# Two attention blocks on one core: K and V issued once per batch step, wq in blocks of columns, Q in half-octet blocks, 97 remainder tiles transposed by DMA

## The chip, the cores and the metric

The kernel runs on one core of a Trainium2 chip. The metric is device time in microseconds (us) of one execution. Before the change three runs took 774.91, 777.09 and 790.09 us; the median is 777.09. The profiled execution took 776.1 us.

## The reference

Two independent problems, A and B, have the same shapes, and their outputs are joined along the last axis. For each:

```python
B, Sq, D = 16, 80, 576
Hq, Hkv, Sk, Dh = 32, 16, 512, 128          # two query heads share a K/V head
q = (x @ wq).reshape(B, Sq, Hq, Dh).transpose(0, 2, 1, 3)
scores = einsum("bhqd,bhkd->bhqk", q, repeat(k_cache, 2)) * Dh ** -0.5
o = einsum("bhqk,bhkd->bhqd", softmax(scores), repeat(v_cache, 2))
out = o.transpose(0, 2, 1, 3).reshape(B, Sq, Hq * Dh) @ wo
```

All inputs are bf16.

## The kernel before

**Units.** The work is cut into 128 units U, 64 for each problem. A unit is one batch element with four K/V heads, that is eight query heads. Eight units that share the same columns of wq and the same half of the batch make an "octet" (`goct`, 16 of them). The two query heads of a K/V head give 160 query rows. 128 of these make one full tile, and the 32 rows that are left over from each of the four heads are put together into one "remainder" tile of 128 rows. So a unit has five score tiles of 128 x 512: one remainder tile (k = 0) and four full ones (k = 1 to 4).

**The steps of a unit.** TensorE projects Q for a whole octet: for each of eight heads, five chained matmuls over the 576 input columns (line 566), for 480 and for 160 columns in turn (`QB = ((0, 6), (6, 2))`, line 520). ACT or DVE evicts and scales the result to qT (lines 577, 578). Scores come from line 689 (full tiles) and line 675 (remainders: four matmuls of 32 columns beside each other in the array, two units at a time). Then DVE takes the negative maximum of each row (698), ACT the exponential with the row sums (702), DVE the reciprocal (708), and POOL normalises in place (711). TensorE transposes the probabilities in four blocks (717), and DVE evicts them to pT (723 for remainders, 725 for full tiles). TensorE multiplies with V (762), ACT evicts to oT (778). The output projection (815) runs over 16 heads at a time in two groups of eight matmuls, and its sums go through `acc` (827, 835) to the output tile (843) and out (849).

**Remainders by DMA.** For some units, listed by ranges in `RSEL` (line 54), the remainder tile isn't transposed by TensorE: SP issues a DMA transpose from p_sb to pT (line 729). Each range of `RSEL` is (first unit, end, which of U mod 4). In this kernel these are 75 of 128 units. There the remainder gets a reciprocal of its own (`RG`, line 53), ahead of the one for the four full tiles.

**Loads.** K is loaded and transposed by DMA from SP (641), into five buffers (`NK`). V is loaded from ACT's queue (645), into four buffers (`NV`); the first four come from SP. wq comes in pieces from SP (539, 542), into two slots; wo comes from SP (606), in four pieces for each half of its columns. x of problem A is loaded (478) and transposed on TensorE (493); x of B is transposed by DMA (512), one of five chunks at a time. SP also stores the output.

**What sets the order.** Nothing is ordered by hand. Every step is an operation of a planner (`_Sched`, lines 117 to 350) with a key, a stream, a duration and the resources that it reads and writes. The planner (`arrange`, line 161) walks through time with its own durations and DMA costs, takes for each engine the ready operation with the lowest priority number, and so fixes each engine's program, the banks of PSUM, and which of ACT and DVE evicts Q. Options of an operation that matter here: `ahead` lowers the priority number, `after` and `lag` hold an operation back in the plan until some time after a "mark" (the PV step of a unit and head; mark 4U + g is head g of unit U) was planned. These holds are only the plan's. In the program that comes out (`finalize`, line 284) an instruction waits only for the semaphores of the data and buffers that it uses; but each engine, SP included, runs its program strictly in order.

**Names that the change touches.** `LA` (line 14) is how many score tiles the scores run ahead of the transposes. `NPA` and `NPR` are the numbers of probability buffers for full and for remainder tiles. `QL0`, `QL1`, `QL2` are how many units the projection of an octet leads its use. `NQ` is the number of octets for which qT has room. `RDK`, `RDO` place the DMA transposes of remainders in SP's order. `WQR`, `XR`, `WOR` place the loads of wq, x of B and wo. `NWARM2` is the number of dummy matmuls (line 453) between the first and the second block of x at the start.

Of the kernel before, what the change touches and what calls it, by code (L numbers as in the profile page):

```python
# [6 lines left out]
BF16 = mybir.dt.bfloat16  # L7
# [5 lines left out]
GR = 2  # L13
LA = 10
NK = 5
NV = 4
NPA = 8
NPR = 4
NPT = 3
NS = 16  # L20
QL0 = 15.0
QL1 = 10.0
KC = 2.1
VK = 8.0
# [16 lines left out]
VN = 1  # L41
VLAG = 2.0
VAF = (None, None, None, None)
STENG = "sp"
# [3 lines left out]
NVS = 4  # L48
# [16 lines left out]
OPSPLIT = 2  # L65
XLD = ((-100.0, -60.0), (-25.0, -24.9))
XH = 0.0
WQ1 = -16.8
WQ1B = 0.02
# [3 lines left out]
LPC = 29.0  # L73
WOR = (((4.0, 1.5), (12.0, 1.5)), ((9.5, 2.0), (17.0, 1.0)), ((9.5, 2.0), (17.0, 1.0)), ((9.5, 2.0), (17.0, 1.0)))
WQR = (-12.0, 2.0)
XR = (-14.0, 2.0)

# [39 lines left out]
class _Sched:  # L117
# [43 lines left out]
    def arrange(self):  # L161
# [72 lines left out]
        while left:  # L234
# [118 lines left out]
def bass_concat_heads__gqa_block_cached__gqa_block_cached__near_ridge_kernel(  # L353
# [27 lines left out]
    with ExitStack() as es:  # L381
# [91 lines left out]
        for half in range(NPP):  # L473
            x_ap = probs[0][0]
            for part, (k0, k1) in enumerate(XP):
                def em_ldx(e, x_ap=x_ap, half=half, k0=k0, k1=k1):
                    src = x_ap.rearrange("b s d -> (b s) d")[half * NROW + k0 * 128:half * NROW + k1 * 128, :]
                    return e.dma_start(xs[:, half * NRT + k0:half * NRT + k1, 0:D],
                                       src.rearrange("(k p) d -> p k d", p=128))

                S.add("sp", XLD[half][part], em_ldx,
                      writes=[R(("xs", half * NRT + k_), 0) for k_ in range(k0, k1)], dsem="d_x%d%d" % (half, part),
                      name="ldx%d.%d" % (half, part), stream="x", dur=0.5, cost=XC * (k1 - k0))
            for blk in range(NRT):
                rb = half * NRT + blk
                vb = S.bank("M0" if half == 0 else "M1")
                x = (XA + 0.5 * blk if blk < 2 else XA + 4.0 + 0.5 * blk) if half == 0 else XH + 0.8 * blk

# [30 lines left out]

        QB = ((0, 6), (6, 2))  # L520
        for goct in range(NG):
# [3 lines left out]
            wsl = wv % 2  # L525
            qsl = goct % NQ
            u0 = goct * 8
            pieces = () if half else ((0, 512), (512, 1024)) if goct < 2 else ((0, 1024),)
            for pi, (c0, c1) in enumerate(pieces):
                st0 = u0 - lead[goct]  # L530
                t_ld = 5.0 * st0 - 20.0 if goct > 1 else (-90.0, WQ1)[goct] + (10.0, WQ1B)[goct] * pi
                fr = (c1 - c0) / 1024.0
                dsem = "d_wqs" if goct == 0 and pi == 0 else "d_wqt" if goct == 1 and pi == 0 else "d_wq%d" % wsl
                eng = ("act", "sp")[goct] if goct < 2 else WENG
                strm = "wqa" if goct == 0 else "wqs" if goct == 1 else "wq"
                for k0, k1 in (((0, 4), (4, 5)) if goct < 2 else ((0, 1), (1, 2), (2, 3), (3, 4), (4, 5))):
                    def em_ldw(e, wq_ap=wq_ap, q=q, wsl=wsl, c0=c0, c1=c1, k0=k0, k1=k1):
                        if k0 == 4:
                            return e.dma_start(wq_sb[64:128, wsl, 4, c0:c1],
                                               wq_ap[512:576, q * 1024 + c0:q * 1024 + c1])  # L540
                        src = wq_ap[k0 * 128:k1 * 128, q * 1024 + c0:q * 1024 + c1]
                        return e.dma_start(wq_sb[:, wsl, k0:k1, c0:c1], src.rearrange("(c p) n -> p c n", p=128))

                    S.add(eng, t_ld + 0.01 * k0, em_ldw,
                          writes=[R(("wq", wsl, ck, p_), wv) for ck in range(k0, k1)
                                  for p_ in ([pi] if len(pieces) == 2 else [0, 1])], dsem=dsem,
                          name="ldw%d.%d.%d" % (goct, pi, k0), stream=strm, dur=0.5,
                          cost=(0.12 + 0.2 * WQC * (k1 - k0) if k0 < 4 else 0.4) * fr,
                          after=int(4 * (st0 + WQR[0] + WQR[1] * k0)) if goct > 1 else None,
                          lag=WLAG if goct > 1 else 0.0)  # L550

            for i in range(8):
                for c in range(2):
                    if goct == 0:
                        b0, nb = ((0, 2), (2, 6))[c]
                        x = -LA - ((6.0, 3.6), (1.2, 0.5))[i // 4][c] + (0.6 if i < 4 else 0.05 if c == 0 else 1.2) * (i % 4)
                    else:
                        b0, nb = QB[c]
                        x = 5.0 * (u0 - lead[goct] + i) + (3.6 if c == 0 else 1.6)
                    n0, n1 = b0 * SQ, (b0 + nb) * SQ  # L560
# [11 lines left out]

                    def em_qev(e, en, qsl=qsl, b0=b0, nb=nb, n0=n0, n1=n1, col=col, vb=vb):
                        dst = qT[:, qsl, b0:b0 + nb, col:col + 80]
                        src = ps[:, vb.phys, 0:n1 - n0].rearrange("p (b s) -> p b s", b=nb)
# [5 lines left out]
                    if prob:  # L581
                        xr += [R(("xT", half, "t", ck), 1) for ck in range(1, 5)]
                    S.add("pe", x, em_qp,
                          reads=[R(("wq", wsl, ck, i // 4), wv) for ck in range(5)] + [R(("wqz",), 0)] + xr,
                          writes=[R(vb, 0)] + [R(("qT", qsl, bl, i), goct) for bl in range(b0, b0 + nb)],
                          name="qp%d.%d.%d" % (goct, i, c), stream="Q",
                          dur=_mm(5, n1 - n0), lat=0.2, alloc=[vb])
                    big = n1 - n0 > 200
                    S.add(("act", "dve"), x + 0.4, em_qev, reads=[R(vb, 0)],
                          writes=[R(("qT", qsl, bl, i), goct) for bl in range(b0, b0 + nb)],  # L590
                          name="qev%d.%d.%d" % (goct, i, c), stream="qev",
# [40 lines left out]
        for U in range(NSU):  # L632
# [3 lines left out]
            _, kc_ap, vc_ap, _, _ = probs[prob]  # L636
            ks, vs, pts, qsl = U % NK, U % NV, U % NPT, goct % NQ

# [16 lines left out]
            rdma = any(a_ <= U < b_ and U % 4 in m_ for a_, b_, m_ in RSEL)  # L655
            for k in range(5):
# [11 lines left out]
                if k == 0:  # L668
                    group.append((U, vb, ks, qsl, bl, goct))
                    if len(group) == gsize[U]:  # L670
                        def em_qkr(e, group=tuple(group)):
                            last = None
                            for _, vb_, ks_, qsl_, bl_, _ in group:
                                for g4 in range(4):
                                    last = e.matmul(ps[32 * g4:32 * g4 + 32, vb_.phys, :],  # L675
                                                    lhsT=qT[:, qsl_, bl_, g4 * 160 + 128:g4 * 160 + 160],
                                                    rhs=kT[:, ks_, :, g4 * 128:(g4 + 1) * 128],
# [3 lines left out]
                        S.add("pe", Qof[(group[0][0], 0)] - LA + 0.0, em_qkr,  # L681
                              reads=[R(("qT", g_[3], g_[4], i), g_[5]) for g_ in group for i in (1, 3, 5, 7)]
                              + [R(("kT", g_[2]), g_[0]) for g_ in group],
# [3 lines left out]
                else:  # L687
                    def em_qk(e, gl=gl, vb=vb, ks=ks, qsl=qsl, bl=bl):
                        return e.matmul(ps[:, vb.phys, :], lhsT=qT[:, qsl, bl, gl * 160:gl * 160 + 128],  # L689
                                        rhs=kT[:, ks, :, gl * 128:(gl + 1) * 128], start=True, stop=True)  # L690

                    S.add("pe", tq, em_qk,
                          reads=[R(("qT", qsl, bl, 2 * gl), goct), R(("qT", qsl, bl, 2 * gl + 1), goct),
                                 R(("kT", ks), U)],
# [234 lines left out]
```

## Time and profile before

| what | value |
|---|---|
| median of three runs | 777.09 us |
| profiled execution | 776.1 us, of which the profile's span is 774.4 us |
| TensorE (PE) busy | 767.0 us, 7,958 matmuls |
| DVE busy | 682.7 us |
| ACT busy | 605.9 us |
| POOL busy | 433.3 us |
| moved by DMA | 170.36 MB, a mean of 220 GB/s |
| remainder transposes by DMA | 75 |

The span runs from the first to the last instruction; the time of the execution has 1.7 us more around it. An engine's busy time counts each moment once, in which at least one of its instructions runs. Matmuls overlap in their pipeline, so the sum of their durations is larger than the busy time; what a matmul costs is read from the distance between two starts. A line such as L717 is line 717 of the kernel. In a timeline, "x4" stands for four instructions merged into one line, with the start of the first and the time to the end of the last.

### The profile page before, as it was taken

To read this page: it belongs to the slowest core of one execution; us is meant where nothing else is said; L and a number is where in the kernel's file an instruction comes from. 1 tells how busy PE (TensorE), PEld (TensorE's weight loads), DVE (VectorE), ACT (ScalarE), POOL (GpSimd) and SP (SyncE) were. 2 spreads that over 40 slices of the span, in tenths; PEclk is the share of its full clock that TensorE was granted. 3 is DMA by queue.
4 is the path that set the end of the run, shared out by engine and by line. 5 is a ranking of instruction groups with operands and counts; after the bars stand their busy time and mean duration, and the time that the engine had idled before them with its cause. 6 is when DMAs were issued, how large, how long until landed. Compare 5 with 4: busy or idle time off the path is not lost.

```text
span 774.4 us, 21088 instructions
## 1 busy us (share of the span) xinstructions
PE 767.0 (99%) x7958; PEld 560.4 (72%) x7958; DVE 682.7 (88%) x1590; ACT 605.9 (78%) x1704; POOL 433.3 (56%) x647
## 2 busy tenths in 40 slices
PE   9999999999999999999999999999999999999998
PEld 5577677777767677777777777677777777767786
DVE  4999989888898989989898899988888888999982
ACT  1778978888888888777777777878788877887860
POOL 1465656566655556555655555655556565565660
PEclk9999999999999999999999999999999999999999
DMA  9998999999999999999999999999999989999931
GB/s 252 225 252 192 252 250 237 230 195 233 205 210 208 220 265 247 267 269 223 200 214 187 206 224 246 249 239 235 218 220 211 200 202 209 246 239 259 249 84 31
DMA packets 411811, 170.36 MB, mean 220 GB/s; under 512 B 317632, under 2 KB 408256, under 8 KB 411712
## 3 DMA queue, kind: packets, MB, share of 16 engines
q1 hardware_dynamic: 345024, 102.83, 74.8%
q10 hardware_dynamic: 66688, 66.20, 28.8%
q8 instruction: 64, 1.05, 0.6%
q14 instruction: 35, 0.29, 0.1%
HBM read 87.46 MB, written 2.95 MB: 117 GB/s over the span
## 4 chain that ended last, share of the span: by engine, by line
PE 88%; DVE 10%; ACT 1%; issue 0%; POOL 0%; ACTq 0%
PE ps L566 20%; PE ps L815 20%; PE ps L762 16%; PE ps L717 14%; PE ps L689 12%; DVE negmax L698 6%; PE ps L675 4%; DVE pT L725 2%; DVE qT L578 1%; ACT p_sb L702 1%; PE ps L438 0%; DVE pT L723 0%; PE ps L453 0%; PE ps L493 0%; DVE xT L497 0%
## 5 line engine op out<-in xcount | busy, mean ns | idle before, releaser
L711 POOL TENSOR_SCALAR p_sb<-p_sb,rinv 128x512 bf16<-128x512 bf16 x640 | 430.9, 695 | 319.9 <-DVE rinv L708 319.8
L702 ACT ACTIVATE p_sb<-ps,negmax 128x512 bf16<-128x512 f32 x640 | 441.4, 693 | 92.7 <-DVE negmax L698 79.9
L698 DVE TENSOR_REDUCE negmax<-ps 128x1 f32<-128x512 f32 x640 | 427.9, 678 | 11.5 <-PE ps L689 7.0
L725 DVE COPY pT<-ps 128x512 bf16<-128x512 bf16 x512 | 209.4, 411 | 20.1 <-PE ps L717 19.2
L762 PE MATMUL ps<-pT,v_sb 128*128 128x160 bf16 x2048 | 219.9, 233 | 1.1 <-issue 0.4
L717 PE MATMUL ps<-ident,p_sb 128*128 128x128 bf16 x2260 | 218.0, 219 | 2.0 <-POOL p_sb L711 1.1
L566 PE MATMUL ps<-xT,wq_sb 128*128 128x480 bf16 (+1 forms) x1280 | 213.0, 300 | 0.1
L762 PEld LDWEIGHTS ps<-pT,v_sb 128*128 128x128 bf16 x2048 | 159.0, 98 | 51.5 <-ACT oT L778 4.5
L689 PE MATMUL ps<-kT,qT 128*128 128x512 bf16 x512 | 190.4, 379 | 0.0
L717 PEld LDWEIGHTS ps<-ident,p_sb 128*128 128x128 bf16 x2260 | 159.5, 98 | 40.1 <-DVE pT L725 7.5
L815 PE MATMUL ps<-wo_sb,oT 128*128 128x288 bf16 x1280 | 171.2, 286 | 0.2
L566 PEld LDWEIGHTS ps<-xT,wq_sb 128*128 128x128 bf16 x1280 | 106.7, 98 | 62.7 <-DVE qT L578 2.7
L815 PEld LDWEIGHTS ps<-wo_sb,oT 128*128 128x128 bf16 x1280 | 122.2, 98 | 36.2 <-issue 1.5
L778 ACT CAST oT<-ps 128x320 bf16<-128x320 f32 x256 | 108.8, 425 | 28.2 <-PE ps L762 27.7
L702 ACT ACTIVATION_READ_ACCUMULATOR p_sb<-ps,negmax 128x1 f32 x640 | 129.1, 202 | 0.0
L578 DVE TENSOR_SCALAR qT<-ps 128x480 bf16<-128x480 f32 (+1 forms) x129 | 71.6, 555 | 17.1 <-PE ps L566 15.7
L577 ACT ACTIVATE qT<-ps 128x160 bf16<-128x160 f32 (+1 forms) x127 | 48.0, 378 | 27.7 <-PE ps L566 27.0
L689 PEld LDWEIGHTS ps<-kT,qT 128*128 128x128 bf16 x512 | 49.4, 98 | 4.5 <-ACT p_sb L702 2.1
L843 DVE TENSOR_TENSOR osb<-ps,acc 128x288 bf16<-128x288 f32 x40 | 18.2, 455 | 25.1 <-PE ps L815 24.5
L675 PE MATMUL ps<-kT,qT 128*32 128x512 bf16 x512 | 39.6, 384 | 0.1
L708 DVE RECIPROCAL rinv<-rowsum 128x4 f32<-128x4 f32 (+2 forms) x203 | 33.0, 165 | 5.1 <-ACT p_sb L702 5.0
L723 DVE COPY pT<-ps 128x512 bf16<-128x512 bf16 x53 | 21.9, 413 | 3.4 <-PE ps L717 3.2
(19 smaller groups left out, 48.5 us busy)
## 6 DMA issues: line engine op xcount, KB each, us to landing
v_sb<-in_B_v_cache_dram ACTq DMA_DIRECT2D x64, 512.0 KB, 5.1
v_sb<-in_A_v_cache_dram ACTq DMA_DIRECT2D x60, 512.0 KB, 5.3
wo_sb<-in_A_wo_dram SPq DMA_DIRECT2D x16, 288.0 KB, 4.5
wo_sb<-in_B_wo_dram SPq DMA_DIRECT2D x16, 288.0 KB, 5.2
wq_sb<-in_B_wq_dram SPq DMA_DIRECT2D x16, 256.0 KB, 5.5
out_dram<-osb SPq DMA_DIRECT2D x40, 72.0 KB, 3.5
v_sb<-in_A_v_cache_dram SPq DMA_DIRECT2D x4, 512.0 KB, 5.3
wq_sb<-in_A_wq_dram SPq DMA_DIRECT2D x8, 256.0 KB, 5.4
```

The source lines that it names most:

```text
L566: last = e.matmul(ps[:, vb.phys, 0:n1 - n0], lhsT=wq_sb[:, wsl, ck, i * 128:(i + 1) * 128], rhs=xT[:, half, ck, n0:n1], start=(ck == 0), s ...
L578: return e.tensor_scalar(dst, src, SCALE, None, op0=AluOpType.mult)
L675: last = e.matmul(ps[32 * g4:32 * g4 + 32, vb_.phys, :], lhsT=qT[:, qsl_, bl_, g4 * 160 + 128:g4 * 160 + 160], rhs=kT[:, ks_, :, g4 * 128: ...
L689: return e.matmul(ps[:, vb.phys, :], lhsT=qT[:, qsl, bl, gl * 160:gl * 160 + 128], rhs=kT[:, ks, :, gl * 128:(gl + 1) * 128], start=True, ...
L698: return e.tensor_reduce(negmax[:, si:si + 1], ps[:, vb.phys, :], axis=AX.X, op=AluOpType.max, negate=True)
L702: return e.activation(p_sb[:, psl, :], ps[:, vb.phys, :], AF.Exp, bias=negmax[:, si:si + 1], scale=1.0, accum_out=rowsum[:, ss, k:k + 1])
L711: return e.tensor_scalar(p_sb[:, psl, :], p_sb[:, psl, :], rinv[:, ss, k:k + 1], 1.0, op0=AluOpType.mult, op1=AluOpType.mult)
L717: last = e.transpose(psb[:, vt.phys, j * 128:(j + 1) * 128], p_sb[:, psl, j * 128:(j + 1) * 128], ident[:])
L725: return e.tensor_copy(pT[:, pts, :, 0:4, gl * 32:gl * 32 + 32], psb[:, vt.phys, 0:512].rearrange("p (j h c) -> p j h c", j=4, h=4))
L762: last = e.matmul(ps[:, vo.phys, off:off + 160], lhsT=v_sb[:, vs, gl, j * 128:(j + 1) * 128], rhs=pT[:, pts, j, :, gl * 32:gl * 32 + 32], ...
L778: return e.copy(dst, src)
L815: last = e.matmul(ps[:, vb.phys, 0:DC], lhsT=oT[:, hi, rb * 128:(rb + 1) * 128], rhs=wo_sb[:, hi, c3 * DC:(c3 + 1) * DC], start=(hi == 0), ...
```

## The change

- **Look-ahead and buffers.** `LA` goes from 10 to 13 score tiles, with two more buffers for full probability tiles and one more for remainders.
- **K and V.** Each unit's K load is held in the plan until the mark that lies 27 heads before the unit's first PV step (`KPH`, from unit 10 on), and each V load until the one 11 heads before (`VPH`, from unit 14 on). So they are planned once per unit, instead of as soon as a buffer is free.
- **wq.** From the third octet on, a load of wq comes as four blocks of 256 columns with all four full row chunks, plus one piece for the last 64 rows. Before, it came as four row chunks with all 1,024 columns, plus the same piece. Dependencies follow the blocks of columns, so a block can be replaced as soon as its two heads are projected.
- **Order with reserves.** In the plan, a DMA counts as landed later than before by a fixed reserve (`XM`: 6.0 for wo and wq, 4.0 for remainder transposes, 3.0 for x, 2.0 for K and V). The priorities `PTO`, `OEO`, `OVO`, `QEO`, `RCO`, which were 0, get values (`QEO` is used nowhere).
- **Q.** An octet is projected in two blocks of four units (320 columns each) instead of six and two units; the second block follows the first by at least 0.7 units. qT has five half-octet blocks instead of three octets.
- **Remainders.** `RSEL` now names 97 units: the odd ones of units 18 to 23 are new, the odd ones now go through from 46 to 61, and from 62 to 125 it is every unit (22 more in all).
- **Start.** The second warm-up has four matmuls instead of eight, and the first transposes of x stand closer together.

The diff, cut to its core:

```diff
-LA = 10
+LA = 13
-NPA = 8
-NPR = 4
+NPA = 10
+NPR = 5
-QL1 = 10.0
+QL1 = 11.0
-QL2 = 10.0
+QL2 = 10.3
-NQ = 3
+NQB = 5
+QSH = 0.7
+QS0 = 12.0
-NWARM2 = 8
+NWARM2 = 4
+VPH = 11
+VU0 = 14
+KPH = 27
+KU0 = 10
+KLAG = 0.0
+XM = dict(wo=6.0, wq=6.0, wqb=6.0, RT=4.0, V=2.0, K=2.0, x=3.0)
-RSEL = ((24, 46, (0, 1, 2, 3)), (46, 50, (1, 3)), (62, 70, (1, 3)), (70, 76, (0, 1, 2, 3)), (76, 94, (1, 3)), (94, 126, (0, 1, 2, 3)))
+RSEL = ((18, 24, (1, 3)), (24, 46, (0, 1, 2, 3)), (46, 62, (1, 3)), (62, 126, (0, 1, 2, 3)))
-RDK = 3.0
-RDO = 6.0
+RDK = 2.0
+RDO = 10.0
-PTO = 0.0
-OEO = 0.0
-OVO = 0.0
-QEO = 0.0
-RCO = 0.0
+PTO = 1.0
+OEO = 4.0
+OVO = 8.0
+QEO = 6.0
+RCO = 2.0
...
-                o.done = t_ + DLAT
+                o.done = t_ + DLAT + XM.get(o.stream, 0.0)
...
-        qT = sb("qT", [128, NQ, 8, 640], BF16)
+        qT = sb("qT", [128, 4 * NQB, 640], BF16)
...
-        QB = ((0, 6), (6, 2))
+        def qpos(goct, bl):
+            return (2 * goct + bl // 4) % NQB * 4 + bl % 4
+
+        QB = ((0, 4), (4, 4))
...
-                for k0, k1 in (((0, 4), (4, 5)) if goct < 2 else ((0, 1), (1, 2), (2, 3), (3, 4), (4, 5))):
+                if goct < 2:
+                    parts = ((0, 4, c0, c1), (4, 5, c0, c1))
+                else:
+                    parts = tuple((0, 4, 256 * j, 256 * j + 256) for j in range(4)) + ((4, 5, 0, 1024),)
...
-                          after=int(4 * (st0 + WQR[0] + WQR[1] * k0)) if goct > 1 else None,
+                          after=int(4 * (sp_ + at)) if goct > 1 else None,
...
-                        x = 5.0 * (u0 - lead[goct] + i) + (3.6 if c == 0 else 1.6)
+                        x = 5.0 * (u0 - lead[goct] + i + c * max(QSH, lead[goct] - QS0)) + 1.6
...
-                  dsem="d_k%d" % ks, name="ldk%d" % U, stream="K", dur=1.8, cost=KC, xp=True)
+                  dsem="d_k%d" % ks, name="ldk%d" % U, stream="K", dur=1.8, cost=KC, xp=True,
+                  after=4 * U - KPH if U >= KU0 else None, lag=KLAG if U >= KU0 else 0.0)
...
-                      lag=VLAG if U >= NVS else 0.0, after=VAF[U] if U < 4 else None)
+                      lag=VLAG if U >= NVS else 0.0, after=VAF[U] if U < 4 else 4 * U - VPH if U >= VU0 else None)
```

More of the change, by code (lines that the diff above doesn't have):

```diff
@@ L67 @@
 XH = 0.0
+XB = 4.0
 WQ1 = -16.8
@@ L482, in bass_concat_heads__gqa_block_cached__gqa_block_cached__near_ridge_kernel @@
                       writes=[R(("xs", half * NRT + k_), 0) for k_ in range(k0, k1)], dsem="d_x%d%d" % (half, part),
-                      name="ldx%d.%d" % (half, part), stream="x", dur=0.5, cost=XC * (k1 - k0))
+                      name="ldx%d.%d" % (half, part), stream="x0", dur=0.5, cost=XC * (k1 - k0))
             for blk in range(NRT):
@@ L535, in bass_concat_heads__gqa_block_cached__gqa_block_cached__near_ridge_kernel @@
                 strm = "wqa" if goct == 0 else "wqs" if goct == 1 else "wq"
-                for k0, k1 in (((0, 4), (4, 5)) if goct < 2 else ((0, 1), (1, 2), (2, 3), (3, 4), (4, 5))):
-                    def em_ldw(e, wq_ap=wq_ap, q=q, wsl=wsl, c0=c0, c1=c1, k0=k0, k1=k1):
-                        if k0 == 4:
[L539 to L548, printed above, removed]
-                          after=int(4 * (st0 + WQR[0] + WQR[1] * k0)) if goct > 1 else None,
+                sp_ = st0 if goct < 2 else u0 - 16 - lead[goct - 2] + max(QSH, lead[goct - 2] - QS0)
@@ L589, in bass_concat_heads__gqa_block_cached__gqa_block_cached__near_ridge_kernel @@
                     S.add(("act", "dve"), x + 0.4, em_qev, reads=[R(vb, 0)],
-                          writes=[R(("qT", qsl, bl, i), goct) for bl in range(b0, b0 + nb)],
+                          writes=[R(("qT", qpos(goct, bl), i), goct) for bl in range(b0, b0 + nb)],
                           name="qev%d.%d.%d" % (goct, i, c), stream="qev",
@@ L681, in bass_concat_heads__gqa_block_cached__gqa_block_cached__near_ridge_kernel @@
                         S.add("pe", Qof[(group[0][0], 0)] - LA + 0.0, em_qkr,
-                              reads=[R(("qT", g_[3], g_[4], i), g_[5]) for g_ in group for i in (1, 3, 5, 7)]
+                              reads=[R(("qT", g_[3], i), g_[4]) for g_ in group for i in (1, 3, 5, 7)]
                               + [R(("kT", g_[2]), g_[0]) for g_ in group],
```

43 lines of the change are left out of this document (26 added, 17 removed).

## The prediction

> **What bounds the kernel now.** I read the page's busy times and chain first, then the groups by line, the waits, stretches of 20 us, and the timelines of TensorE and of SP's queue.
>
> ```profile
> PE 767.0 (99%) x7958; PEld 560.4 (72%) x7958; DVE 682.7 (88%) x1590; ACT 605.9 (78%) x1704; POOL 433.3 (56%) x647
> ...
> PE 88%; DVE 10%; ACT 1%; issue 0%; POOL 0%; ACTq 0%
> ```
>
> TensorE is busy nearly always and carries the chain. Busy could still hide slack, so look at the distances between starts:
>
> ```profile
> 107.53 0.44 PE L762 MATMUL ps<-pT,v_sb 128*128 128x160 bf16 x4
> 107.81 0.39 PE L717 MATMUL ps<-ident,p_sb 128*128 128x128 bf16 x4
> 108.03 0.44 PE L762 MATMUL ps<-pT,v_sb 128*128 128x160 bf16 x4
> 108.31 0.39 PE L717 MATMUL ps<-ident,p_sb 128*128 128x128 bf16 x4
> 108.53 0.38 PE L689 MATMUL ps<-kT,qT 128*128 128x512 bf16 x1
> ```
>
> The columns are start, length and matmuls. A group of four transposes starts 0.22 us before its successor: 55.7 ns a matmul, 128 columns at 2.4 a ns plus some 2.5. Of 160 columns one takes 69 ns, of 288 122, of 480 202, of 512 216: all pure streaming. Added up by form, all 7,958 starts account for 754 of the 770 us between the first and last start (two 0.1 us turns per remainder group included). So only some 16 us are left to win: 3 before the second block of x, and 13 in all that follows. Of those 13, gaps over 0.1 us make 8.4. What they look like:
>
> ```profile
> 543.64 0.44 PE L762 MATMUL ps<-pT,v_sb 128*128 128x160 bf16 x4 [0.20 <-issue]
> ```
> ```profile
> 495.98 0.40 PE L717 MATMUL ps<-ident,p_sb 128*128 128x128 bf16 x4 [0.23 <-DVE pT L725]
> 496.21 0.38 PE L689 MATMUL ps<-kT,qT 128*128 128x512 bf16 x1
> 496.43 0.72 PE L762 MATMUL ps<-pT,v_sb 128*128 128x160 bf16 x8
> 497.45 0.40 PE L717 MATMUL ps<-ident,p_sb 128*128 128x128 bf16 x4 [0.31 <-POOL p_sb L711]
> ```
>
> The first is a PV that waits for a remainder tile transposed by DMA (unit 89; it landed at 543.55). The others wait for pT's eviction and for a probability tile that POOL had just normalised. Why was the DMA late? SP's queue, with the length of each issue:
>
> ```profile
> 527.12 6.45 SPq L641 DMA_TRANSPOSE kT<-in_B_k_cache_dram  x1
> 533.62 0.58 SPq L542 DMA_DIRECT2D wq_sb<-in_B_wq_dram  x1
> 534.25 4.73 SPq L641 DMA_TRANSPOSE kT<-in_B_k_cache_dram  x1
> 539.08 1.21 SPq L729 DMA_TRANSPOSE pT<-p_sb  x1
> ```
>
> Unit 89's buffer was free at 530.26, but SP stood for 4 to 6 us on each K load's issue and reached the transpose at 539.08. The rings are nearly full here. What they can move:
>
> ```profile
> 280.00:300.00 20.00, 20.00 (x213) 14.78 (x211) 17.99 (x42) 16.94 (x49) 12.17 (x19) 1.00 1.15 265
> 300.00:320.00 20.00, 19.92 (x221) 14.57 (x214) 19.30 (x47) 17.01 (x48) 11.19 (x18) 1.00 1.19 261
> 320.00:340.00 20.00, 20.00 (x213) 14.93 (x212) 18.32 (x41) 16.02 (x46) 12.62 (x19) 1.00 1.19 281
> ...
> 520.00:540.00 20.00, 20.00 (x215) 14.87 (x213) 16.59 (x40) 15.59 (x44) 12.42 (x19) 1.00 1.11 237
> 540.00:560.00 20.00, 19.80 (x215) 14.75 (x214) 17.84 (x42) 15.97 (x46) 10.12 (x15) 1.00 1.15 229
> ```
>
> The last column is GB/s: 269 over 280 to 340 with PE untroubled. The granted clock, third from last, is 1.00. DMA is the second bound, and the change leans on it.
>
> **Part by part.** The base is the profiled run's 776.1 us (span 774.4); the median of the three runs is 1.0 higher.
>
> *Remainder tiles by DMA, 75 to 97.* 22 groups of four transposes leave TensorE: 22 x 0.223 = **-4.9 us**, all in the bound. The Trainium skill's "TensorE: Matmul & The Clock Gate" (Back-to-back issue gap) gives about 81 ns a matmul at 128 columns in a stream with weight loads; by that it would be -7.1, but the trace shows 55.7 ns. DVE loses 22 evictions (413 ns, -9.1) and gains 22 reciprocals (some 0.16, +3.5); DVE idles 92 us in all, so nothing. SP gains 22 issues of 1.21 us and the rings 22 x 131 KB, mostly in units 62 to 94 (13) and 46 to 62 (6); priced under the rival.
>
> *Warm-up, 8 to 4 matmuls.* The eight (L453) take 2.31 us, four 0.9 to 1.1. But the second block of x lands at 7.55, the transposes behind the warm-up now start at 8.06: **-0.45**.
>
> *Q in half-octet blocks.* A head was 5 x (202.5 + 69) ns; it becomes 5 x 2 x 136, interpolated for 320 columns: 1.36 us both times, **0**. Evictions, between the rows of 160 and 480 columns (DVE 312 and 652 ns, ACT 301 and 570): DVE 127 x 0.48 = 61 after 71.5, ACT 129 x 0.435 = 56 after 48. Even at the 480 row both stay under 92% and inside their idle time: 0. qT has room for 20 unit blocks instead of 24; a block's last projection still streams over 1 us before its first use, as before: 0.
>
> *Look-ahead 10 to 13, more p buffers.* In the stream a score's transpose now stands a median of 13.2 us behind it, not 10.3 (lowest 6.9, not 6.6, in unit 0). Max, exp, reciprocal and normalising take a median 6.5, 95% 8.5. So the four waits at 81.5, 83.0, 496.0 and 497.5 (0.45, 0.48, 0.41, 0.48) go: **-1.8**. A remainder's scores stand 13.3 or more ahead of its PV, not 11.6, and its DMA is placed earlier on SP; the waits at 258.0, 269.7, 543.6 and 688.3 (0.41, 0.59, 0.37, 0.36) go: **-1.7**. Late next are K loads.
>
> *Order of K, V, wq.* The clock is no wait: it only orders SP's and ACT's programs, and each issue still waits for its buffer. V goes out about half a unit (2.9 us) later; V lands 6.5 us or more before use, so 0 under that cover. Were it gone, each late V would cost its lateness. On ACT the later place makes a blocking wait for PV rarer; queued behind one are the exps and Q evictions. A wq block is 256 KB either way, and wq lands 6 us or more ahead: 0, bounded by a few tenths for one late block. At the start K1 to K3 go ahead of V0, but qkr needs them 1.4 us sooner: K1 landed at 20.6 and is now needed near 21, K3 near 24.6 about when it lands. From 0 to 2; I take **+0.5**, and **+0.5** for new small waits on the busier rings.
>
> Sum: 776.1 - 4.9 - 0.45 - 1.8 - 1.7 + 1.0 = **768.3 us**.
>
> **Rivals.**
> *Waits only move.* Other gaps replace the 3.5 us: 776.1 - 5.35 = 770.8, to 774 with 2 us more at the start. For it: DVE is full from 20 to 80 us (19.96, 19.27, 19.57 of 20), where deeper look-ahead adds no throughput.
>
> *The rings become the bound (the other side).* Place: units 76 to 94. In the new order that stage issues 23.1 MB besides remainders (18 K and 19 V of 524 KB, six wo, eight wq, two stores) and 18 remainder transposes, before 10. It took 105 us; 103 would be left. At 269 GB/s the 23.1 MB need 86 us, so it decides at (103 - 86)/18 = 0.94 us a transpose. The price is not in the trace alone: below, its bytes at 269 GB/s, 0.49; above, 1.2, SP's issue and about the shortest issue-to-landing seen. I take 0.75, because units 94 to 112 already run 18 of 18 this way and K issues there are shortest (median 2.6 against 3.8 in 76 to 94): 86 + 13.5 fits in 103. At 1.2 the stage is over by 4.6 us. If the rings also hold only 252 GB/s (mean of the seven stretches 280 to 340 and 480 to 560), 76 to 94 is over by 10.4, 24 to 46 by 3.9, 46 to 62 by 5.3: 767.3 + 19.6 = 787. Against so much: by the same price 24 to 46 of before would need 128.5 us and took 126.5 without loss. Half of it, 777, is likelier. The Trainium skill's "DMA: Bandwidth & Descriptors" speaks against the change: under Measured it wants transfers of 1 MiB, and its table (64 KB in 0.95 us, 1 MB in 6.15, on another issue path) makes an estimated 1.3 us for 128 KB; by that the stage would be 6 us over. No row here isolates it.
>
> *Waits all but vanish.* The 8.4 us of gaps over 0.1 us go and only the smaller ones stay: 776.1 - 5.35 - 8.4 = 762.4; a shade more is over 2%. Against it: the DVE-bound start stays.
>
> **How the numbers follow.** Forecast 0.58 (764 to 772), waits move 0.15, rings 0.20, waits vanish 0.07. About 2% (15.5 us of 777.1) is what a measurement of this kernel tells from no change: under 761.6 is faster (part of the last and of the forecast's low side, 0.05), over 792.6 slower (the rings with losses beyond the price above, 0.08), the rest 0.87. The range, 761.5 to 783, leaves out part of the last and the rings' upper half.
>
> **What would show it.** L717 with x2172 and the transposes to pT x97; L566 one form, near 136 ns apart; no PV ended by a late DMA; TensorE's waits on L717 fewer. If rows with 76 to 94 (about 480 to 570 us) show PE under 19.5 of 20, score matmuls waiting for kT and longer K issues, the rings are the bound and I am wrong; if gaps at 20 to 35 us grow, it was the start.

## The result, and the profile after

| | before | after |
|---|---|---|
| median of 20 runs each (lowest to highest) | 778.4 us (774.3 to 793.9) | 774.0 us (767.9 to 784.2) |
| ratio, 95% interval | | 0.9936 [0.9909, 0.9962] |
| profiled execution, span | 776.1 us, 774.4 | 776.2 us, 774.4 |

The medians are of all runs; a ratio leaves out executions more than 1.5% above the fastest of their kernel, three of the changed kernel's twenty and two of the kernel before's. The change gains 0.64%, about 5 us, where 8.8 us against the median shown (1.1%) was forecast. The profiled execution of the changed kernel is one of its longer ones, and as long as that of the kernel before, so it shows more of what goes wrong than a typical one.

The page after, answering to the busy times and the chain shown before:

```profile
span 774.4 us, 20988 instructions
...
PE 758.1 (98%) x7866; PEld 572.9 (74%) x7866; DVE 671.1 (87%) x1588; ACT 608.7 (79%) x1706; POOL 434.1 (56%) x647
...
PE 96%; DMA 1%; ACT 1%; issue 1%; DVE 0%; SPq 0%
```

TensorE is busy 9 us less in the same span: work has left it, and idle time has taken its place. It still carries 96% of the chain; what is new there is 1% of DMA. The groups by form show that the intended work did leave (columns: instructions, busy time, mean ns of one, idle time ahead):

```profile
L733 PE MATMUL ps<-ident,p_sb 128*128 128x128 bf16 x2172 | 207.2, 219 | 0.0
L581 PE MATMUL ps<-xT,wq_sb 128*128 128x320 bf16 x1200 | 202.3, 300 | 0.7 <-ACT p_sb L718 0.6
...
L592 ACT ACTIVATE qT<-ps 128x320 bf16<-128x320 f32 x126 | 55.1, 437 | 22.3 <-PE ps L581 22.0
L593 DVE TENSOR_SCALAR qT<-ps 128x320 bf16<-128x320 f32 x114 | 54.8, 482 | 9.8 <-PE ps L581 8.9
```

L733 is the old L717: 88 matmuls fewer, four for each of 22 remainders. Q has its 320-column form, and its evictions take 437 and 482 ns. The two spans are equal. Each splits into what the starts of the matmuls account for at their streaming distances (from one start to the next where nothing waits), the waits (starts that come more than 0.1 us later than that, by the granted clock), and the time lost to a lower granted clock (us):

| | streaming | waits before 40 us | ended by a late DMA | other waits | clock | rest |
|---|---|---|---|---|---|---|
| before | 754.4 | 2.1 | 1.9 | 4.5 | 0 | 11.5 |
| after | 748.7 | 4.0 | 10.4 | 0.8 | 1.7 | 8.8 |
| after minus before | -5.7 | +1.9 | +8.5 | -3.7 | +1.7 | -2.7 |

In this execution the late DMAs ate the gain: 8.5 us are waits for four remainder tiles (units 49, 84, 86 and 89) and 1.9 for a K load (unit 93). They lie in two stages: units 46 to 62 (4.8 us of waits, 0.4 before) and units 76 to 94 (5.8, 1.4 before). Stretches of 20 us of the changed kernel (busy time of PE, PEld, DVE, ACT, POOL, then clock, DMA share and GB/s):

```profile
280.00:300.00 20.00, 20.00 (x224) 15.45 (x222) 18.41 (x44) 17.63 (x52) 13.12 (x20) 1.00 1.10 228
300.00:320.00 20.00, 15.41 (x148) 11.20 (x146) 13.94 (x33) 12.95 (x36) 8.81 (x14) 0.91 1.23 219
500.00:520.00 20.00, 18.65 (x192) 13.66 (x190) 17.42 (x40) 16.52 (x49) 10.86 (x17) 1.00 1.16 225
520.00:540.00 20.00, 19.36 (x202) 14.94 (x201) 16.99 (x41) 14.60 (x42) 10.82 (x17) 1.00 1.09 234
540.00:560.00 20.00, 16.93 (x175) 12.46 (x173) 14.24 (x34) 13.37 (x38) 10.09 (x16) 1.00 1.08 230
```

PE stands under 19.5 in four of the five stretches, with 219 to 234 GB/s moved. For three of them, units 76 to 94, that is the sign that the prediction named for the rings (its word for the DMA queues with the engines that serve them); the fourth belongs to units 46 to 62. TensorE's timeline of the changed kernel at its largest wait:

```profile
302.78 0.39 PE L733 MATMUL ps<-ident,p_sb 128*128 128x128 bf16 x4
307.76 0.44 PE L778 MATMUL ps<-pT,v_sb 128*128 128x160 bf16 x4 [4.59 <-issue]
```

And its SP queue ahead of that (start, length of the issue):

```profile
292.55 4.43 SPq L656 DMA_TRANSPOSE kT<-in_A_k_cache_dram  x1
297.02 0.60 SPq L554 DMA_DIRECT2D wq_sb<-in_B_wq_dram  x1
297.66 3.34 SPq L656 DMA_TRANSPOSE kT<-in_A_k_cache_dram  x1
301.10 1.22 SPq L745 DMA_TRANSPOSE pT<-p_sb  x1
302.36 0.58 SPq L557 DMA_DIRECT2D wq_sb<-in_B_wq_dram  x1
302.99 6.69 SPq L656 DMA_TRANSPOSE kT<-in_A_k_cache_dram  x1
```

The PV of unit 49 needs the remainder tile issued at 301.10, which landed at 307.67. Its buffer was free at 292.72, just after SP had begun a K load that took 4.43 us to issue; another K and a block of wq followed before SP came to it. This is the pattern of unit 89 in the kernel before, with a longer wait. In units 76 to 94 it builds up: from unit 82 to unit 88 a transpose is issued 1.6, 4.5, 6.8, 10.3, 10.5, 10.9 and 11.5 us after its data and buffer are ready.

### The profile page after: what moved, and what is told of

The parts are those of the page before. It is cut to its first block, busy times and chain, and to the rows that moved or that the text cites. A ratio compares the mean times of both kernels' runs of the same rounds, so it can differ in the third digit from the quotient of the medians.

```text
span 774.4 us, 20988 instructions
## 1 busy us (share of the span) xinstructions
PE 758.1 (98%) x7866; PEld 572.9 (74%) x7866; DVE 671.1 (87%) x1588; ACT 608.7 (79%) x1706; POOL 434.1 (56%) x647
## 4 chain that ended last, share of the span: by engine, by line
PE 96%; DMA 1%; ACT 1%; issue 1%; DVE 0%; SPq 0%
PE ps L581 23%; PE ps L831 20%; PE ps L778 19%; PE ps L733 16%; PE ps L705 14%; PE ps L691 4%; ACT p_sb L718 1%; DMA acc<-in_A_x_dram 1%; DMA pT<-p_sb 1%; PE ps L502 0%; DVE negmax L714 0%; ACT oT L794 0%; DVE qT L593 0%; SPq L487 0%; DVE osb L859 0%
## 5 line engine op out<-in xcount | busy, mean ns | idle before, releaser
L741 DVE COPY pT<-ps 128x512 bf16<-128x512 bf16 x512 | 207.9, 412 | 20.3 <-PE ps L733 17.8
L581 PE MATMUL ps<-xT,wq_sb 128*128 128x320 bf16 (+2 forms) x1280 | 213.7, 300 | 0.7 <-ACT p_sb L718 0.6
L733 PE MATMUL ps<-ident,p_sb 128*128 128x128 bf16 x2172 | 207.2, 219 | 0.0
L778 PEld LDWEIGHTS ps<-pT,v_sb 128*128 128x128 bf16 x2048 | 164.1, 98 | 54.0 <-issue 6.4
L733 PEld LDWEIGHTS ps<-ident,p_sb 128*128 128x128 bf16 x2172 | 154.9, 98 | 34.3 <-issue 5.9
L581 PEld LDWEIGHTS ps<-xT,wq_sb 128*128 128x128 bf16 x1280 | 116.8, 98 | 53.5 <-ACT oT L794 5.1
L592 ACT ACTIVATE qT<-ps 128x320 bf16<-128x320 f32 (+1 forms) x129 | 56.0, 434 | 31.5 <-PE ps L581 31.1
L593 DVE TENSOR_SCALAR qT<-ps 128x320 bf16<-128x320 f32 (+2 forms) x127 | 61.7, 487 | 13.1 <-PE ps L581 12.1
L724 DVE RECIPROCAL rinv<-rowsum 128x1 f32<-128x1 f32 (+2 forms) x225 | 36.7, 163 | 4.3 <-ACT p_sb L718 4.3
L843 ACT COPY acc<-ps 128x288 f32<-128x288 f32 x40 | 16.0, 399 | 4.2 <-PE ps L831 3.3
```

Of the source, the lines that this page charges most:

```text
L581: last = e.matmul(ps[:, vb.phys, 0:n1 - n0], lhsT=wq_sb[:, wsl, ck, i * 128:(i + 1) * 128], rhs=xT[:, half, ck, n0:n1], start=(ck == 0), s ...
L593: return e.tensor_scalar(dst, src, SCALE, None, op0=AluOpType.mult)
L733: last = e.transpose(psb[:, vt.phys, j * 128:(j + 1) * 128], p_sb[:, psl, j * 128:(j + 1) * 128], ident[:])
L741: return e.tensor_copy(pT[:, pts, :, 0:4, gl * 32:gl * 32 + 32], psb[:, vt.phys, 0:512].rearrange("p (j h c) -> p j h c", j=4, h=4))
L778: last = e.matmul(ps[:, vo.phys, off:off + 160], lhsT=v_sb[:, vs, gl, j * 128:(j + 1) * 128], rhs=pT[:, pts, j, :, gl * 32:gl * 32 + 32], ...
```

## The experiments

Two theories stood against each other. R, the rings: a transpose by DMA costs more than the 0.75 us taken, and 97 of them overfill two stages, 46 to 62 and 76 to 94. O, the order: the new places of K, V, wq and the transposes in SP's and ACT's programs make transfers late, whatever their number. The first six kernels ask which of the two, the later ones how they meet. Numbers are medians in us (lowest to highest, runs), and ratios to the kernel before, which ran beside each. Medians of different experiments were taken at different times, so kernels are compared by their ratios; the changed kernel's is 0.9936. "The new order" stands for all of the change but the list of remainders, "the old order" for the kernel before; late DMAs and waits are counted as in the table above, in one profiled execution each.

**1. The old list of remainders in the new order.**

```diff
-RSEL = ((18, 24, (1, 3)), (24, 46, (0, 1, 2, 3)), (46, 62, (1, 3)), (62, 126, (0, 1, 2, 3)))
+RSEL = ((24, 46, (0, 1, 2, 3)), (46, 50, (1, 3)), (62, 70, (1, 3)), (70, 76, (0, 1, 2, 3)), (76, 94, (1, 3)), (94, 126, (0, 1, 2, 3)))
```

> The changed kernel with the old list of 75 remainder transposes by DMA, all else changed. Theory R (the rings are full in units 46 to 50 and 76 to 94, and the 22 added transposes overfill them): PV and score waits that end with a DMA's landing fall from 9.8 us in the changed kernel's profile to 3 or less, TensorE does 4.9 us more, so about 772 us against some 778 of before. Theory O (the new order of K, wq and transposes on SP makes them late, however many there are): the waits stay near 9 us, and the time is 779. Theory S (late transfers in the profile were chance, the missing part is at the start): no such waits, yet 779, since 774 plus 4.9 is left.

Measured: 774.4 (770.2 to 780.1, 12), 0.9971 [0.9936, 1.0006]. Streaming is back at 753.6, so 22 transposes are worth 4.9 us, as the sum had it. Late transposes all but vanish (0.4 us), but 7.1 us of the profiled execution, its longest, are waits for K loads (units 21, 23, 53 and 89). So the new order alone neither wins nor loses much; with 75 tiles there is slack for the transposes, not for every K.

**2. The new list in the old order**, `RSEL` of the changed kernel in the kernel before.

```diff
-RSEL = ((24, 46, (0, 1, 2, 3)), (46, 50, (1, 3)), (62, 70, (1, 3)), (70, 76, (0, 1, 2, 3)), (76, 94, (1, 3)), (94, 126, (0, 1, 2, 3)))
+RSEL = ((18, 24, (1, 3)), (24, 46, (0, 1, 2, 3)), (46, 62, (1, 3)), (62, 126, (0, 1, 2, 3)))
```

> The kernel before with only the new list of 97 remainder transposes. Theory R: waits that end with a late transfer rise from 1.7 to over 5 us, in units 46 to 62 and 76 to 94, and eat the 4.9 us that TensorE saves: 777 to 782 us, ratio to before 0.998 to 1.005. Theory O and theory S: the 4.9 us show, 773.5 us, ratio 0.994.

Measured: 786.1 (781.0 to 790.9, 6), 1.0125 [1.0075, 1.0176]. Late DMAs make 16.2 us, and the clock loses 6.8, in its longest execution. The tiles alone are a loss of over 1%: it takes the rest of the change to turn them into a gain.

**3. wq by rows of 128 with all 1,024 columns**, in the changed kernel.

```diff
-parts = tuple((0, 4, 256 * j, 256 * j + 256) for j in range(4)) + ((4, 5, 0, 1024),)
+parts = tuple((j, j + 1, 0, 1024) for j in range(5))
```

> The changed kernel with wq again loaded as four row chunks of 128 x 1024 (runs of 2 KB) and one of 64 rows, issued once the slot's last projection is done, instead of four blocks of 256 columns (runs of 512 B). If the blocks' short runs are what overfills the rings (theory W): late-transfer waits fall to half or less and the time to 770 us. Theory R: the bytes are the same, waits stay near 9 us in the profile and the time within 1.5 us of the changed kernel's 774.

Measured: 777.0 (771.6 to 802.2, 13), 1.0000 [0.9968, 1.0031]: by the ratios some 5 us above the changed kernel, with a wide scatter. Its buffers also come free later and its places in SP's order move, so this doesn't separate the form from the order; run 6 does for the form.

**4. The transposes thinned to every other unit in 76 to 94** (88 tiles).

```diff
-RSEL = ((18, 24, (1, 3)), (24, 46, (0, 1, 2, 3)), (46, 62, (1, 3)), (62, 126, (0, 1, 2, 3)))
+RSEL = ((18, 24, (1, 3)), (24, 46, (0, 1, 2, 3)), (46, 62, (1, 3)), (62, 76, (0, 1, 2, 3)), (76, 94, (1, 3)), (94, 126, (0, 1, 2, 3)))
```

> The changed kernel with only the odd units' remainders by DMA in units 76 to 94: 88 transposes, nine fewer. Theory R: TensorE does 2.0 us more, and the waits in 76 to 94 (1.5, 1.4 and 1.9 us, and 0.8 behind them) nearly all go, so 770 to 772 us; the wait in unit 49 stays. Theories O and S: 774 plus 2.0, 776 us.

Measured: 768.4 (766.2 to 781.5, 12), 0.9901 [0.9869, 0.9933]. TensorE does nine groups (2.0 us) more, and still the kernel is some 3 us faster than with 97 tiles (0.9901 against 0.9936; the intervals overlap). Waits in 76 to 94 are gone; of late DMAs 3.6 us are left, 3.3 of them again at unit 49.

**5. Thinned in 46 to 62 as well** (none in 46 to 50: 86 tiles).

```diff
-(46, 62, (1, 3)), (62, 76, (0, 1, 2, 3)), (76, 94, (1, 3))
+(50, 62, (1, 3)), (62, 76, (0, 1, 2, 3)), (76, 94, (1, 3))
```

> The changed kernel with odd units only in 76 to 94 and no remainders by DMA in units 46 to 49: 86 transposes. Theory R (the rings are overfull in two places): the wait in unit 49, 4.8 us in the changed kernel's profile and 3.4 in the thinned one's, goes too; TensorE does 0.4 us more than in the thinned kernel (768.4 us), so 765 to 768. If that wait was chance, or another late transfer takes its place: 769 to 771.

Measured: 767.1 (766.5 to 771.5, 6), 0.9886 [0.9847, 0.9924]. This is 1.1% below the kernel before, the forecast's size, and 0.5% below the changed kernel: the intervals overlap a little, but its longest execution is shorter than the changed kernel's median. Stretches of 20 us of this kernel, with the columns as before:

```profile
300.00:320.00 20.00, 20.00 (x218) 15.30 (x216) 19.87 (x48) 17.35 (x49) 13.02 (x20) 1.00 1.16 273
500.00:520.00 20.00, 20.00 (x219) 15.25 (x218) 17.74 (x43) 15.86 (x44) 11.21 (x17) 1.00 1.21 249
540.00:560.00 20.00, 20.00 (x215) 15.11 (x214) 17.29 (x42) 15.44 (x45) 11.49 (x18) 1.00 1.04 200
```

PE is full again in the three stretches that had lost most, DMA carries no late transfer after 40 us, and its six runs lie within 5 us, where the changed kernel's twenty spread over 16.

**6. The transfers by themselves.** SP and ACT run stages of 24 steps with the kernel's buffers and nothing else: K and V; the same with one remainder transpose per step (KVR); with two; with 256 KB of wq as a row block (w); as a column block (c); K alone; transposes alone.

```diff
+PHASES = ("KV", "KVR", "KVRR", "KVw", "KVc", "K", "R")
```

> No computation, only transfers, in seven stages of 24 steps, each step waiting for its buffers: K+V; K+V and one remainder transpose; K+V and two; K+V and 256 KB of wq as 128 rows of 2 KB; K+V and 256 KB of wq as a block of 256 columns; K alone; remainder transposes alone. The output is zeros. My sum had K+V at 3.9 us a step (269 GB/s), 0.75 us more for a transpose, and 1.0 for either form of wq. Theory R: a transpose costs 0.94 us or more beside K+V. If it costs 0.5 to 0.75 the rings had room for 18 of 18 units, and something else made them late. Theory W: the block of columns costs 0.4 us or more above the rows.

Measured in its one run of 702.3 us, the seven stages from SP's first issue to the last landing (the columns are POOL's busy time, clock, DMA share, GB/s):

```profile
2.30:92.40 90.10, 0.00 (x0) 1.00 1.17 279
92.50:219.80 127.30, 0.00 (x0) 1.00 1.14 223
220.40:366.30 145.90, 0.00 (x0) 1.00 0.93 215
367.90:479.10 111.20, 0.00 (x0) 1.00 1.09 282
480.50:593.10 112.60, 0.00 (x0) 1.00 1.12 278
594.30:658.10 63.80, 0.00 (x0) 1.00 1.09 197
658.30:690.80 32.50, 0.00 (x0) 1.00 0.48 97
```

Divided by 24, a step takes 3.75 us with K and V, and 5.30 with one remainder transpose: it costs **1.55 us** beside K and V, above the forecast's bound of 1.2. A second adds only 0.78, and alone one takes 1.35. With transposes among them the rings move 223 GB/s, not 279, at nearly the same DMA share (1.14 and 1.17), so a price by bytes could not find this. A block of wq costs 0.88 us by rows and 0.94 by columns: the form hardly matters. Three cautions. In these stages V also waits for the K, and K for the V, of four steps back, where the kernel's loads wait for TensorE to free their buffers, so a price can hold some of that coupling. The first stage's first V went out 1.6 us ahead of SP's first issue; counted from there, a step is 3.82 and a transpose 1.49. And SP's issue is most of a transpose's 1.35 alone (1.26), so how much of the 1.55 is SP's issue and how much the rings isn't separated.

By these prices, units 76 to 94 need per unit 3.75 for K and V, 10/18 x 1.55 for transposes and 14/18 x 0.91 for wo and wq blocks (both priced as wq): 5.3 us before, in 105/18 = 5.8. With 18 transposes it is 6.0 in 103/18 = 5.7: over by 0.3 a unit, some 5 us in the stage. Its waits were 5.8 in the profiled execution. Units 94 to 112, which had all their remainders by DMA already, need 3.75 + 1.55 + 4/18 x 0.91 = 5.5 in the same 5.7 and fit, as they ran without loss.

**7. Look-ahead and p buffers near the old ones, with 97 tiles.**

```diff
-LA = 13
-NPA = 10
-NPR = 5
+LA = 11
+NPA = 8
+NPR = 4
```

> The changed kernel with a look-ahead of 11 score tiles instead of 13, and 8 and 4 probability buffers as before. My prediction gives the look-ahead 1.8 us at transposes and a part of 1.7 at late remainders. If so, waits for POOL and for pT come back (over 1 us at unit 8 to 94), remainder transposes have 2 us less room, and the time is 2 to 5 us above the changed kernel's 774. If the look-ahead gives nothing: 774.

Measured: 783.8 (777.6 to 789.7, 9), 1.0076 [1.0037, 1.0115]: some 10 us slower than with 13. The profile has 12.6 us of late DMAs (10.4 with 13); waits for POOL are back (1.7 us), and a transpose's landing leads its use by a median of 5.2 us instead of 6.4. So look-ahead and buffers are worth much more than the 1.8 us of waits that they remove from TensorE. That they let each transpose go out earlier is a part of it; how large a part, one profile doesn't settle.

**8. Every unit from 24 to 125** (105 tiles).

```diff
-(24, 46, (0, 1, 2, 3)), (46, 62, (1, 3)), (62, 126, (0, 1, 2, 3))
+(24, 126, (0, 1, 2, 3))
```

> The changed kernel with every unit's remainder by DMA from 24 to 126: 105 transposes, eight more, all in units 46 to 62. TensorE does 1.8 us less. Theory R: waits for late transposes and K in 46 to 62 rise by over 5 us, the time to 777 or more. Theories O and S: 772.

Measured: 780.3 (773.2 to 789.2, 12), 1.0026 [0.9996, 1.0056]. Streaming falls by another 1.8 us, and the time rises by some 7 over the changed kernel's.

**9. V two heads later.**

```diff
-VPH = 11
+VPH = 9
```

> The changed kernel with V planned two heads later (9 heads before a unit's first PV instead of 11). V lands many us before its use while K and remainder transposes land late, so V's share of the rings is taken too early. Theory P (bursts: the rings could serve in time if V gave way): late K and transposes shrink, the time falls by 2 us or more below the changed kernel's. Theory R (the sum is over what the rings move, whoever goes first): within 1.5 us of it, or slower where V then comes late itself.

Measured: 780.7 (777.1 to 798.5, 12), 1.0038 [1.0005, 1.0071]. Two heads later costs about 1%. The profiled execution shows it in small pieces only (8.1 us late DMAs, 3.3 other waits, 5.1 clock), none of them a wait for V, so why it costs isn't shown.

**10. The changed kernel again**, unedited.

> The changed kernel itself, to compare in the same runs: 774, ratio to before 0.994. In its profile theory R expects late transposes or K loads in units 46 to 62 and 76 to 94 again, from 5 to 12 us in all; if such waits were chance they move elsewhere.

Measured: 774.4 (767.1 to 782.4, 12), 0.9940 [0.9906, 0.9974]. The PV of unit 49 is late again, by 6.3 us: in all seven profiles of the new order with 88 to 105 tiles it waits, for 1.6 to 6.3 us, so that place is the kernel's. None of the waits of units 76 to 94 is there: the stage takes 103.0 us instead of 108.7, with 18 transposes that are issued up to 7.0 us after they are ready and still land in time. So this stage is at its limit, and whether it goes over it varies by execution; that the price of run 6 comes so near to the 5.8 us is in part chance.

**11. The 86 tiles of run 5 in the old order.**

```diff
-RSEL = ((24, 46, (0, 1, 2, 3)), (46, 50, (1, 3)), (62, 70, (1, 3)), (70, 76, (0, 1, 2, 3)), (76, 94, (1, 3)), (94, 126, (0, 1, 2, 3)))
+RSEL = ((18, 24, (1, 3)), (24, 46, (0, 1, 2, 3)), (50, 62, (1, 3)), (62, 76, (0, 1, 2, 3)), (76, 94, (1, 3)), (94, 126, (0, 1, 2, 3)))
```

> The kernel before with only the thinned list of 86 remainder transposes that the fastest version so far (767.1 us, ratio 0.989) has. If the list alone makes the gain: 768, ratio 0.99. If it takes the look-ahead and the new order as well, as the 786 us of the kernel before with 97 transposes say: TensorE saves 2.5 us, waits for late transfers take them back, 774 to 779, ratio 0.998 to 1.005.

Measured: 787.3 (782.3 to 792.7, 6), 1.0128 [1.0078, 1.0177]: 2.4% above the same list in the new order, 20 us between the medians. All of the change but the list is left out here, not the places of the loads alone. TensorE in this kernel, and, in the second view, SP's queue ahead of it:

```profile
499.97 0.38 PE L689 MATMUL ps<-kT,qT 128*128 128x512 bf16 x1
505.49 1.23 PE L762 MATMUL ps<-pT,v_sb 128*128 128x160 bf16 x8 [5.14 <-issue]
```

```profile
486.64 9.05 SPq L641 DMA_TRANSPOSE kT<-in_B_k_cache_dram  x1
495.79 1.30 SPq L729 DMA_TRANSPOSE pT<-p_sb  x1
```

SP stands on the issue of a K load for 9.05 us, with unit 81's transpose, ready since 488.61, behind it. At the start of a stage of run 6, with no other transfer in flight yet, such an issue takes 1.30 us.

**12. Run 5 with the smaller look-ahead.**

```diff
-LA = 13
-NPA = 10
-NPR = 5
+LA = 11
+NPA = 8
+NPR = 4
```

> The fastest version (86 transposes, 767.1 us) with a look-ahead of 11 score tiles and 8 and 4 probability buffers. Theory R alone (with a list that the rings can carry nothing is late): only the small waits for POOL and pT come back, 767 to 770. Theory L (look-ahead is what lets late transfers pass unseen; a remainder's scores stand 12.1 us ahead of its PV at least, not 13.3, and a median of 19.7, not 22.2): waits for transposes of 5 us or more, 774 or more.

Measured: 772.0 (767.7 to 775.7, 12), 0.9930 [0.9898, 0.9962]: 0.4% above run 5 by the ratios, whose intervals overlap, and 5 us between the medians; with 97 tiles it cost 1.4%. Only 1.5 us are late DMAs; waits for POOL and pT are back (3.4 us).

**13 to 15. Run 5 without the holds on K and V, without V's, and without K's from unit 44 on.**

```diff
-VU0 = 14
-KU0 = 10
+VU0 = 1000
+KU0 = 1000
```

> The fastest version (86 transposes, 767.1 us) without the plan's hold on K and V: K and V are planned as soon as their buffers are free. If the clock matters (theory C): late K loads or transposes of 4 us or more, 772 or more. If the list and the look-ahead do it all: 767, within 1.5 us.

```diff
-VU0 = 14
+VU0 = 1000
```

> The fastest version with the hold on K kept and that on V left out. Theory V: 780 or more, with V issued a median of 2 us after its buffer is free (5.6 in the fastest version) and K and transposes late. Theory K: 767 to 771.

```diff
-after=4 * U - KPH if U >= KU0 else None, lag=KLAG if U >= KU0 else 0.0)
+after=4 * U - KPH if KU0 <= U < 44 else None, lag=KLAG if KU0 <= U < 44 else 0.0)
```

> The fastest version (86 transposes, 767.1 us) with the hold on V kept, and that on K only up to unit 43. Without the hold on V alone it was 776.3, without both 790.5. Theory K (the hold keeps K from standing ahead of the remainder transposes on SP): transposes late by 4 us or more in units 46 to 94, 775 or more. If only V's hold counts: 767 to 770.

Measured: without both 790.5 (780.0 to 795.3, 12), 1.0129 [1.0087, 1.0172]; without V's 776.3 (770.8 to 786.9, 12), 1.0005 [0.9974, 1.0035]; without K's from unit 44 on 779.9 (768.4 to 789.3, 6), 0.9890 [0.9821, 0.9959]. Of the last's six executions three took 768 to 774 us and three, which the ratio leaves out, 785 to 789, so its size stays open. Its profile, of one of the shorter, has 5.8 us of late transposes, where run 5 has none. With the holds the planner also changes the order of TensorE, DVE and ACT a little, so each of these differences is that of a whole program. SP's queue in the kernel without both holds, which does again what run 11 showed:

```profile
484.69 7.51 SPq L656 DMA_TRANSPOSE kT<-in_B_k_cache_dram  x1
492.25 0.60 SPq L554 DMA_DIRECT2D wq_sb<-in_B_wq_dram  x1
492.89 0.58 SPq L865 DMA_DIRECT2D out_dram<-osb  x1
493.51 0.63 SPq L557 DMA_DIRECT2D wq_sb<-in_B_wq_dram  x1
494.24 1.20 SPq L745 DMA_TRANSPOSE pT<-p_sb  x1
```

Unit 81's transpose had its buffer at 488.42 and landed at 502.13, 3.5 us after TensorE had run out of other work. Over the whole kernel, from the profiled executions (us; issue of a remainder transpose after its data and buffer are ready, and how far its landing leads its use):

| 86 tiles | time | issued after ready: median, 90% | lead: median, lowest 10% |
|---|---|---|---|
| run 5, both holds | 767.1 | 0.4, 5.0 | 7.3, 4.1 |
| no hold on V | 776.3 | 0.6, 3.4 | 7.5, 3.9 |
| no holds | 790.5 | 2.9, 8.1 | 5.8, 0.6 |
| old order (run 11) | 787.3 | 2.2, 7.5 | 5.0, 0.1 |

The hold on K, taken away after V's, costs 1.2% by the ratios (1.0005 and 1.0129), some 10 us, and the table shows how: the transposes lose their lead. What V's hold does isn't settled: its kernel's profiled execution is its shortest, and its transposes are on time in it but for 0.5 us; 3.9 us are waits for late K loads (units 25, 91 and 93), where run 5 has none. For a kernel without K's hold from the first unit on, with V's in, there is no time, so K's hold by itself is known only by the open result from unit 44 on.

## Why the prediction was right and wrong

- *22 remainder transposes off TensorE, -4.9 us:* right. Streaming with 75 and with 97 tiles in the same order differs by 753.6 - 748.7 = 4.9. The distance of 55.7 ns a matmul holds.
- *Q in half-octet blocks, 0:* right. The evictions took 482 and 437 ns (0.48 and 0.435 taken), and TensorE waits for them once, for 0.1 us.
- *Warm-up and start, -0.45 and +0.5:* the warm-up went as worked out: the second x block's transposes start at 7.43, not 8.06. The start costs more: waits before 40 us grew from 2.1 to 4.0 with the dummy matmuls gone, so it is about 1 us worse than the sum had it.
- *Look-ahead, -1.8:* right in what it removes: waits for POOL and pT fell from 3.7 to 0.4 us. Runs 7 and 12 show that it is worth more, 1.4% with 97 tiles and about 0.4% with 86; the lead that it gives to transposes by DMA is a part of that.
- *Late remainder DMAs, -1.7, with +0.5 for new small waits on the rings:* **wrong, the first step that failed.** Late DMAs went from 1.9 to 10.4 us in the profiled execution (8.1 in run 10's), and 1.7 us of lower clock followed them. Three of the four waits that were to go went, but unit 89's grew and others came. Behind it is the price of a transpose beside K and V: 0.75 taken, at most 1.2 allowed, some 1.5 measured. The prediction's point of decision was 0.94. Its reason for 0.75, that units 94 to 112 already ran 18 of 18, didn't carry over: in the kernel before, SP issued no wq and four blocks of wo between 582 and 685 us, but eight pieces of wq (two of them of 64 rows) and six of wo in the shorter stretch from 480 to 570.
- *Order of K, V and wq, 0 ("it only orders"):* **wrong, the second step.** The planner's holds add no wait of their own, that much was so. But SP stands on the issue of a K load for up to 9 us, so the order decides what waits behind it. With the same 86 tiles, run 13 leaves out the holds on K and V alone and takes 790.5 us where run 5 takes 767.1, as long as run 11, which leaves out all of the change but the list (787.3). Without this step the 86 transposes make the kernel slower than before.
- *The rival "the rings become the bound" (0.20)* came about in its place, units 76 to 94, and in 46 to 62 too. By the medians about half of the forecast gain is missing, not all of it as at its price of 777 and above. Its sum at 1.2, 4.6 us over in 76 to 94, is near the 5.6 us of late DMAs that the first profile has there; units 24 to 46, where it feared 3.9 us, have none. (Its 787 counts from 767.3, where the sum is 768.3; nothing hangs on that.)

The two errors had opposite signs: that the time still fell inside the range owes something to that, which is luck. Neither theory stands alone. The list without the rest of the change loses (runs 2 and 11), the rest without the list does little (run 1), and lateness comes where a stage's transfers fill its time and SP's order leaves no lead. That thinning two stages restores the forecast's size (runs 4 and 5) shows the load's part, and the prices of run 6 say which stage is at its limit; run 13 shows the order's. The same sum for 46 to 62 isn't closed, since no run prices the x chunks that load there and the stores. The reserves `XM` are without effect: with them left empty the planner gives every engine its operations in the same order, for 97 and for 86 tiles.

The Trainium skill's "DMA: Bandwidth & Descriptors" (Measured) spoke against the change: the estimate from its table, 1.3 us for 128 KB, was nearer to the 1.55 measured than the 0.75 taken from rows of the trace.

## What to carry to other kernels

Price a kind of transfer beside the transfers that it will meet, not by its bytes: a stage of 24 steps of K, V and one more gives it in a single run. Where one queue issues both big loads and small urgent transfers in program order, a load that is issued early can block the urgent one for as long as its issue takes, here up to 9 us instead of 1.3; hold the load back until it is needed, and the small one gets its lead. Then fill each stage only as far as the measured prices fit in its time: 86 tiles beat both 75 and 97 here.

## What the runs showed of the hardware

After a longer wait the granted clock falls to half. Stretches of 3 us of the changed kernel around the wait at unit 49 (clock third from last):

```profile
303.00:306.00 3.00, 0.17 (x4) 0.00 (x0) 1.59 (x4) 1.98 (x6) 2.50 (x4) 1.00 1.35 170
306.00:309.00 3.00, 1.24 (x16) 0.65 (x16) 0.00 (x0) 0.00 (x0) 0.00 (x0) 0.90 1.24 245
309.00:312.00 3.00, 3.00 (x19) 1.82 (x16) 1.68 (x4) 1.27 (x4) 1.35 (x3) 0.53 1.24 227
312.00:315.00 3.00, 3.00 (x35) 2.36 (x33) 2.78 (x7) 2.62 (x8) 2.05 (x4) 1.00 1.24 296
```

From 308.4 to 311.8 us TensorE runs at half speed, which costs 1.7 us more on top of the 4.6 of idle time; in runs 2 and 10 such a stretch also lasted 6.8 us. Over all the profiles of the two kernels and their variants, from 10 us on, 21 idle times of 2.7 to 7.1 us each brought 3.4 or 6.8 us at half speed; none of up to 2.4 us did, nor one of 3.4 us (run 3). The Trainium skill's "TensorE: Matmul & The Clock Gate" (Part 1: The HAM clock gate) states such a fall to half speed after an idle window of about 3.4 us. The traces agree with the length, in that the stretches last 3.4 us or twice that, but six of the falls came after a shorter idle time, 2.7 to 3.3 us. All six executions of run 5, which has no such wait in its profile, have a mean clock of 1.000; the changed kernel's twenty lie between 0.991 and 1.000.

The rings themselves vary from one execution to the next. In run 1, from 100 to 110 us, they moved 101 and 102 GB/s with loads queued, where the changed kernel moved 192 and 233 in the same stretches. Unit 21's K, issued at 107.07 and at 106.93, landed at 125.98 in run 1 and at 119.50 in the changed kernel; the wait for it is 2.25 us. What slowed the rings isn't shown by any run.
